# Retention with a rational feed-forward layer: blocks of one chunk from four batches, and one list schedule for all engines

## The chip, the cores and the metric

The kernel runs on one core of one Trainium2 chip. The metric is the time of one execution on the device in microseconds (us), the median of several runs. Engines are named as in the profile: PE (matrix products; PEld are its weight loads), DVE (vector), ACT (activation), POOL (GpSimd) and SP, which here only issues DMA transfers. Each engine works through its own queue of instructions in order and waits on semaphores for what others produce.

## The reference

Inputs are q, k and v of shape (4 batches, 8 heads, 768 positions, 64), two weight matrices (512 x 2048 and 2048 x 512), four numbers a and two numbers b. All is float32.

```python
for t in range(S):                                  # retention
    state = gamma * state + outer(k[:, :, t], v[:, :, t])
    y[:, :, t] = scale * (q[:, :, t] @ state)
x = y.transpose(0, 2, 1, 3).reshape(B * S, H * D)   # 3072 tokens x 512
h = x @ w_in
P = a[0] + a[1] * h + a[2] * h**2 + a[3] * h**3
Q = 1.0 + abs(b[0]) * abs(h) + abs(b[1]) * h**2
out = (P / (Q + 1e-06)) @ w_out
```

gamma differs by head, scale is 1/8.

## The kernel before, in words

**Retention in chunks.** The 768 positions of a batch are cut into C = 6 chunks of 128. For a chunk, `scores` (products at L254) multiplies k and q, `mask` (L261) multiplies by a causal mask into `aT`, `values_early` and `values_late` (L297, L308) multiply with v, and `recall` (L287) adds what the state of earlier chunks contributes, if there is one. `outer` (L274) makes the chunk's own k-v products and `update` (L317, L319) puts them into the state, which `scale_state` (L224, on POOL) decays. v is scaled by the decay in `scale_v` (L218, on POOL). The result `px` is scaled (L329) and split into a high part `xh` (L330, ACT) and a low part `xl` (L334, DVE), so that float32 accuracy comes out of products of two shorter parts.

**Blocks and slots.** Four consecutive chunks of 128 tokens make a block n of 512 tokens; there are 6 blocks, and 24 chunks numbered batch by batch, so block 0 is the first four chunks of batch 0, and block 1 the last two of batch 0 and the first two of batch 1. The hidden dimension has NF = 16 tiles f of 128. A slot is one pair (n, f), 96 in all: `gemm_in` (L392) makes twelve 128x128x512 products into `ph`; the rational function is worked out on ACT (L403, L409, L411, L420, L421), POOL (L410, sometimes L405) and DVE (L415, L416, L424, L425, L426); `split` (L431, L432) cuts the result into `gh` and `gl`; `gemm_out` (L447) makes twelve products into the four banks `po`. For the first two blocks the hidden tiles are done in two halves, block 0 f 0 to 7, block 1 f 0 to 7, then both again with f 8 to 15; the half sums go to DRAM and come back (`store`, `load_halves`).

**Weights.** 32 weight tiles (w_in and w_out by f) come as 64-bit words and are decoded on the chip: `decode_low` (L130, ACT) fills a buffer `t`, `decode_high` (L138, ACT) a PSUM bank `u`, `decode_join` (L146, L149, DVE) puts them together, `decode_split` (L159, ACT) and `decode_rest` (L166, POOL) make a high and a low part. `t` has three buffers.

**Order.** The order on every engine is written by hand. `opening()` does the first four chunks one after the other, with some products of zeros in between (`fill`, L350), and the first decodes. `run()` then goes through the slots k: the in-products of slot k, the out-products of slot k - 3 (LAG), the rational function of slot k, and in fixed places one decoded tile and a first or second half of a chunk of the next block (`parts`). SP issues loads in an order given by `FIRST`, `FETCH` and the calls of `load_rest`. Chunks 2 and 3 borrow buffers of the feed-forward part, which is not running yet. PSUM has eight banks: two for `ph`, two that scores, px and decodes take in turn, four for `po` (which the opening uses for other things).

Of the kernel before, what the change touches and what calls it, by code (L numbers as in the profile page):

```python
# [18 lines left out]


@with_exitstack
def tile_retention_rational_ffn(
# [9 lines left out]
    par: bass.AP,  # L32
    causal: bass.AP,
    xdec: bass.AP,
    vdec: bass.AP,
    sdec: bass.AP,
# [10 lines left out]
    NB = NSTEP // SPB  # L47

# [4 lines left out]
    ps_o = ctx.enter_context(tc.tile_pool(name="ps_o", bufs=1, space=PSUM))  # L53

    ps = ctx.enter_context(tc.tile_pool(name="ps", bufs=1, space=PSUM))

    o_tiles = {}
    count = {"ph": 0, "bank": 0, "u": 0}
    opened = []

    def bank(name, dtype=F32):
        tag = "ph" if name == "ph" else "bank"
        count[tag] += 1
        return ps.tile([P, TB], dtype, name=name, tag=f"{tag}{count[tag] % 2}")

    def early_bank(name, tag, dtype=F32):
        pool = ps_o if tag.startswith("po") else ps
        return pool.tile([P, TB], dtype, name=name, tag=tag)

    def u_bank():  # L70

        if not opened:
            return early_bank("u", "ph0", U32)
        if len(opened) < 2:
            count["u"] += 1
            return early_bank("u", f"po{count['u'] % 2}", U32)
        return bank("u", U32)

    def px_banks(i):
        if len(opened) < 2:  # L80
            return [early_bank("px", f"po{r + 2 * (i % 2 or i >= SPB)}") for r in range(2)]
        return [bank("px") for _ in range(2)]

# [3 lines left out]
    small = const.tile([P, H + NP + 10], F32, name="small")  # L87
    vdec_sb = small[:, :H]
# [5 lines left out]
    state = const.tile([P, NP, D], F32, name="state")  # L94
    zeros = ff.tile([P, DM], F32, name="zeros", tag="o", bufs=BUFS["o"]).bitcast(BF16)[:, :TB]
    wp = ctx.enter_context(tc.tile_pool(name="wp", bufs=1))
    w1, w2 = {}, {}
# [3 lines left out]
    lead, HF = 4, NF // 2  # L101
    tiles = []
    for h in range(0, NF, HF):
        tiles += [(0, h + f) for f in range(lead)]
        for f in range(h, h + HF):
            tiles += [(1, f)] + [(0, f + lead)] * (f + lead < h + HF)
    raws = []

    def fetch(count=1):
        for m, f in tiles[len(raws) : len(raws) + count]:  # L110
            raw = wp.tile([P, DM, 2], U32, name="raw", tag=f"w{m}_{f}")
            nc.sync.dma_start(
                out=raw.rearrange("p m w -> p (m w)"), in_=(w_in, w_out)[m][f]
            )
            raws.append(raw)

    us, ts = {}, {}

    def decode_read(i):
        decode_low(i)  # L120
        decode_high(i)

    def decode_low(i):
        if i >= len(tiles):
            return


        ts[i] = ff.tile([P, DM], U32, name="t", bufs=3)
        byte = raws[i].rearrange("p m w -> p (m w)").bitcast(U8)[:, 3::8]
        nc.scalar.activation(ts[i], byte, AF.Identity, bias=lcon[:, 0:1], scale=1.0 / 32)  # L130

    def decode_high(i):
        if i >= len(tiles):
            return


        us[i] = u_bank()
        nc.scalar.activation(  # L138
            us[i].bitcast(F32), raws[i][:, :, 1].bitcast(F32), AF.Abs, scale=2.0 ** -112
        )  # L140

    def decode_join(i):
        if i >= len(tiles):
            return
        u = us.pop(i)
        nc.vector.scalar_tensor_tensor(  # L146
            u, u, 3, ts[i], ALU.logical_shift_left, ALU.bitwise_or
        )
        nc.vector.scalar_tensor_tensor(  # L149
            ts[i], raws[i][:, :, 1], 0x80000000, u, ALU.bitwise_and, ALU.bitwise_or  # L150
        )

    def decode_split(i):
        if i >= len(tiles):
            return
        m, f = tiles[i]

        w = (w1, w2)[m][f] = wp.tile([P, 2, DM], F32R, name="w", tag=f"w{m}_{f}")
        nc.scalar.copy(w[:, 0], ts[i].bitcast(F32))  # L159

    def decode_rest(i):
        if i >= len(tiles):
            return
        m, f = tiles[i]
        w = (w1, w2)[m][f]
        nc.gpsimd.tensor_sub(w[:, 1], ts.pop(i).bitcast(F32), w[:, 0].bitcast(F32))  # L166


    steps = {}
    x_tiles = {}  # L170

    def x_block(n):
        if n not in x_tiles:
            x_tiles[n] = (
                xp.tile([P, NP, TB], F32R, name="xh"),
                xp.tile([P, NP, TB], F32R, name="xl"),
            )
        return x_tiles[n]

    borrowed = {2: ("gh", "gh", "q", "gl", "s"), 3: ("gh", "gl", "q", "gl", "s")}

    def landing(i, which, name, shape):
        if i in borrowed:
            tag = borrowed[i][which]
            full = ff.tile([P, TB], F32, name=name, tag=tag, bufs=BUFS.get(tag, 2))
            return full.rearrange("p (a b) -> p a b", b=shape[2])[:, : shape[1]]
        return at.tile(shape, F32, name=name)

    def load_part(i, n, src, which, shape):
        if i < NSTEP:
            st = steps.setdefault(i, {})
# [16 lines left out]

    def scale_v(i):
# [466 lines left out]
```

## Time and profile before

| what | value |
|---|---|
| median of 3 runs | 639.0 us (637.94 to 640.6) |
| profiled execution | 639.73 us, of it 638.0 us from the first to the last instruction (the span) |
| PE busy | 611.7 us (96% of the span), 4506 products |
| DVE, ACT, POOL busy | 452.9, 441.4 and 334.2 us |
| mean granted PE clock | 0.988 |
| moved by DMA | 55.11 MB, 86 GB/s over the span |

The profile is one execution. Its views are: a page with busy times and the costliest groups of instructions; groups by line; the timeline; busy times in chosen stretches of the span, with the PE clock that was granted in them; waits (who waited for whom); and a chain of work followed back from the last instruction. Times are us from the start of the span unless marked ns. A line number is one of the kernel as printed above. PE products overlap each other, and the ends of products are modelled, so the time of a set of products is read best from start to start.

### The profile page before, as it was taken

The page shows a single profiled execution, that of the slowest core. Times are in us where ns is not written, and L with a number is a line of the kernel's source. Part 1 is how long each engine was busy: PE and PEld are TensorE (multiplying, and loading weights), DVE is VectorE, ACT ScalarE, POOL GpSimd, SP SyncE. Part 2 cuts the span into 40 slices and gives each one's busy share as a digit, 9 for nine tenths or more (in the row PEclk, how much of TensorE's full clock was granted, in tenths as well). Part 3 has the DMA queues.
Part 4 walks back from the last instruction along what each step waited for, and adds up shares of the span by engine and source line. Part 5 has one row for each costly group of instructions (what it writes and reads, how often), then busy time and mean ns, then how long its engine had stood idle before and what let it go on. Part 6 is the DMA issues. An engine that isn't in the chain of part 4 may idle for free.

```text
span 638.0 us, 11577 instructions
## 1 busy us (share of the span) xinstructions
PE 611.7 (96%) x4506; PEld 494.4 (77%) x4510; DVE 452.9 (71%) x731; ACT 441.4 (69%) x721; POOL 334.2 (52%) x288
## 2 busy tenths in 40 slices
PE   6766999999999999999999999999999999999997
PEld 4655778888877878788888888888878888888885
DVE  3778688888888666785666777667766766666664
ACT  2488789888886665567666675766766666777773
POOL 1566568887875543454453454535354443444442
PEclk9887999999999999999999999999999999999999
DMA  8995563101015232320120311111311000100001
GB/s 306 393 370 174 192 241 141 44 1 66 1 45 180 87 96 85 124 76 17 59 59 17 116 44 61 48 27 54 112 40 43 2 0 1 42 25 2 0 2 66
DMA packets 27270, 55.11 MB, mean 86 GB/s; under 512 B 3408, under 2 KB 6096, under 8 KB 27216
## 3 DMA queue, kind: packets, MB, share of 16 engines
q1 hardware_dynamic: 27216, 54.38, 25.1%
q8 instruction: 35, 0.57, 0.4%
q14 instruction: 19, 0.16, 0.1%
HBM read 45.98 MB, written 8.39 MB: 85 GB/s over the span
## 4 chain that ended last, share of the span: by engine, by line
PE 67%; ACT 13%; DVE 11%; issue 5%; DMA 2%; POOL 1%; SPq 1%; POOLq 0%; DVEq 0%; ACTq 0%
PE po L447 30%; PE ph L392 30%; ACT t L130 3%; ACT s L420 2%; ACT ph L421 2%; DVE q L424 2%; PE pa L254 2%; DVE p L426 2%; DVE ph L425 2%; PE px L308 2%; DMA v<-in_v 2%; PE px L287 2%; PE px L274 1%; ACT u L138 1%; ACT s L409 1%
## 5 line engine op out<-in xcount | busy, mean ns | idle before, releaser
L410 POOL TENSOR_TENSOR q<-q,s 128x512 f32<-128x512 f32 x96 | 124.4, 1296 | 224.1 <-ACT s L409 215.4
L392 PE MATMUL ph<-xh,w 128*128 128x512 f32 (+2 forms) x776 | 210.4, 393 | 10.1 <-DVE p L426 5.7
L447 PE MATMUL po<-w,gh 128*128 128x512 f32 x768 | 201.4, 394 | 0.0
L392 PEld LDWEIGHTS ph<-xh,w 128*128 128x128 f32 x776 | 143.8, 188 | 42.5 <-DVE t L149 3.0
L447 PEld LDWEIGHTS po<-w,gh 128*128 128x128 f32 x768 | 143.4, 189 | 30.7 <-POOL w L166 0.2
L403 ACT ACTIVATE q<-ph 128x512 f32<-128x512 f32 x96 | 57.2, 596 | 111.3 <-PE ph L392 111.2
L415 DVE TENSOR_TENSOR p<-ph,p 128x512 f32<-128x512 f32 x96 | 66.2, 689 | 94.1 <-ACT p L411 94.1
L432 POOL TENSOR_TENSOR gl<-p,gh 128x512 fp32r<-128x512 f32 x96 | 124.4, 1295 | 9.7 <-ACT gh L431 3.8
L447 PE MATMUL po<-w,gl 128*128 128x512 f32 x384 | 111.1, 391 | 0.2 <-POOL gl L432 0.2
L424 DVE SCALAR_TENSOR_TENSOR q<-q,small,ph 128x512 f32<-128x512 f32 x96 | 71.4, 744 | 47.3 <-ACT ph L421 47.2
L392 PE MATMUL ph<-xl,w 128*128 128x512 f32 (+2 forms) x388 | 104.1, 390 | 0.0
L420 ACT ACTIVATE s<-q,small 128x512 f32<-128x512 f32 x96 | 69.4, 723 | 22.7 <-POOL q L410 22.7
L392 PEld LDWEIGHTS ph<-xl,w 128*128 128x128 f32 x388 | 73.2, 189 | 15.4
L447 PEld LDWEIGHTS po<-w,gl 128*128 128x128 f32 x384 | 72.5, 189 | 15.8 <-POOL gl L432 0.6
L416 DVE SCALAR_TENSOR_TENSOR p<-p,small,ph 128x512 f32<-128x512 f32 x96 | 71.8, 748 | 3.4
L411 ACT ACTIVATE p<-ph,small 128x512 f32<-128x512 f32 x96 | 73.2, 762 | 0.0
L425 DVE SCALAR_TENSOR_TENSOR ph<-p,small,ph 128x512 f32<-128x512 f32 x96 | 72.0, 750 | 0.0
L431 ACT CAST gh<-p 128x512 fp32r<-128x512 f32 x96 | 58.6, 610 | 16.7 <-DVE p L426 16.7
L426 DVE SCALAR_TENSOR_TENSOR p<-q,ph 128x512 f32<-128x512 f32 x96 | 65.9, 687 | 3.3
L409 ACT ACTIVATE s<-q,small 128x512 f32<-128x512 f32 x80 | 65.3, 816 | 2.7
L421 ACT ACTIVATE ph<-s 128x512 f32<-128x512 f32 x96 | 57.8, 602 | 9.9 <-DVE p L416 0.8
L218 POOL TENSOR_TENSOR v<-v,small 128x512 f32<-128x512 f32 x24 | 25.0, 1044 | 41.8 <-DMA v<-in_v 40.1
(41 smaller groups left out, 439.8 us busy)
## 6 DMA issues: line engine op xcount, KB each, us to landing
raw<-in_w_in SPq DMA_DIRECT2D x16, 512.0 KB, 5.7
raw<-in_w_out SPq DMA_DIRECT2D x16, 512.0 KB, 7.3
kT<-in_kT SPq DMA_DIRECT2D x24, 256.0 KB, 2.8
qT<-in_qT SPq DMA_DIRECT2D x24, 256.0 KB, 3.2
v<-in_v SPq DMA_DIRECT2D x24, 256.0 KB, 3.6
out<-o SPq DMA_DIRECT2D x24, 256.0 KB, 2.1
k<-in_k SPq DMA_DIRECT2D x20, 256.0 KB, 3.9
q2T<-in_q2T SPq DMA_DIRECT2D x20, 128.0 KB, 3.2
```

The lines of the kernel that those rows point to most:

```text
L392: nc.tensor.matmul(ph[:, t0:t1], w1[f][:, part, kt * P : (kt + 1) * P], x[:, kt, t0:t1], start=(i == 0), stop=(i == 3 * NP - 1),)
L409: nc.scalar.activation(s, q, AF.Identity, bias=babs[:, 0:1], scale=babs[:, 1:2])
L410: nc.gpsimd.tensor_mul(q, q, s)
L411: nc.scalar.activation(p, ph, AF.Identity, bias=par_sb[:, 2:3], scale=par_sb[:, 3:4])
L416: nc.vector.scalar_tensor_tensor(p, p, par_sb[:, 1:2], ph, ALU.add, ALU.mult)
L420: nc.scalar.activation(s, q, AF.Abs_reciprocal_sqrt, bias=qcon[:, 0:1])
L421: nc.scalar.activation(ph, s, AF.Square)
L424: nc.vector.scalar_tensor_tensor(q, q, qcon[:, 0:1], ph, ALU.add, ALU.mult)
L425: nc.vector.scalar_tensor_tensor(ph, p, par_sb[:, 0:1], ph, ALU.add, ALU.mult)
L426: nc.vector.scalar_tensor_tensor(p, q, 2.0, ph, ALU.subtract, ALU.mult, reverse0=True)
L432: nc.gpsimd.tensor_sub(gl, p, gh.bitcast(F32))
L447: nc.tensor.matmul(o_tiles[n][tt], g_[:, tt * P : (tt + 1) * P], w2[f][:, part], start=(first and m == 0), stop=(last and m == 2),)
```

## The change

1. **Block = the same chunk of four batches.** Chunk number i is now chunk c = i // 4 of batch i % 4. Block 0 holds the four first chunks, which have no state to recall and none of which depends on another; every batch has a state of its own (`state` is four times as large). Block 5 holds the four last chunks. Stores go to the rows of their batch.
2. **First chunks.** The mask for c = 0 (`mask0`, prepared on the host, 128 x 2 x 384) contains the decay and the scale, so `px` needs no scaling there and ACT and DVE split it at once. The outer products of the first chunks are not made with them, but in two steps of two batches each (`first_states`), with a DVE product that contains the decay of the state.
3. **Small inputs** (v's decay, the state's decay, a and b) come in one load.
4. **One list schedule.** Each piece of work is put down as a step with the engines that can do it, a cost in ns, what it comes after, the buffers it takes and uses, and a rank. `Plan.order` then simulates the engines on the host with these costs: it repeatedly takes, of the steps that can begin, the one that begins first, with a look-ahead of 100 to 300 ns on DVE, ACT and POOL within which the lower rank wins, and emits it on its engine. SP's loads are steps too, with a modelled rate and at most eight under way. The ranks are the slot numbers plus an offset for the kind of step, and for chunks and weight tiles a table of numbers; another table ranks the loads. `s` (the former L409 or L405) may go to ACT or POOL in the first 40 slots. In the opening, products of zeros fill modelled gaps of PE over 0.6 us.
5. **Buffers:** `t` has two instead of three; `q2T` one; the others as before.

The heart of the diff (the functions that issue instructions keep their bodies, apart from the points above):

```diff
+class Plan:
...
+    def order(self, emit):
...
+            by_engine = {}
+            for x in open_:
+                t = self.ready(x)
+                if t is None:
+                    continue
+                for e in x.engines:
+                    start = max(t, self.free.get(e, 0))
+                    if e == "SP" and len(self.landings) >= LANES:
+                        start = max(start, self.landings[-LANES])
+                    by_engine.setdefault(e, []).append((start, x))
+            best = None
+            for e, found in by_engine.items():
+                limit = min(f[0] for f in found) + LOOK.get(e, 0)
+                start, x = min((f for f in found if f[0] <= limit), key=lambda f: (f[1].rank, f[0]))
+                if best is None or start < best[0]:
+                    best = start, e, x
...
+            self.commit(x, e, start)
+            emit(x, e, gap)
...
-    def mask(i):
-        st = steps[i]
-        for s in range(2):
-            st["aT", s] = at.tile([P, 2, 3 * D], F32, name="aT")
-            nc.vector.tensor_mul(
-                st["aT", s], st["pa"][s],
-                causal_sb.rearrange("p x t -> p (x t)").unsqueeze(1).broadcast_to([P, 2, 3 * D]),
-            )
...
+            def mask(_, s=s):
+                st.setdefault("aT", {})[s] = at.tile([P, 2, 3 * D], F32, name="aT", bufs=BUFS["aT"])
+                by = causal_sb.rearrange("p x t -> p (x t)").unsqueeze(1).broadcast_to([P, 2, 3 * D])
+                if c == 0:
+                    by = masks[s].rearrange("p (j t) -> p j t", t=3 * D)
+                nc.vector.tensor_mul(st["aT"][s], st["pa"][s], by)
...
+    def first_states(b, rank, gate):
...
+        def run(_):
+            cell["pk"] = psum(pk, 0, "pk").rearrange("p (b h d) -> p b h d", b=2, d=D)
+            for x, st in enumerate((st0, st1)):
+                outer(st, cell["pk"][:, x], x == 0)
...
+        def update(_):
+            for x in range(2):
+                nc.vector.tensor_mul(
+                    state[:, b + x], cell["pk"][:, x],
+                    sdec_sb.unsqueeze(2).broadcast_to([P, NP, D]),
+                )
...
+        L = step(("ACT",), (651, 761), low, [got], rank, [t], kind="low")
+        U = step(("ACT",), (548, 623), high, [got, L], rank, [u], kind="high")
+        J = step(("DVE",), (1300, 1385), join, [L, U], rank, uses=[t, u], kind="join")
+        S = step(("ACT",), (509, 607), split, [J], rank, uses=[t], kind="split")
+        R = step(("POOL",), (1249, 1295), rest, [S], rank, uses=[t], kind="rest")
...
+        engines = ("ACT", "POOL") if k < SHARED else ("ACT",)
...
+        P1 = step(("POOL",), (1250, 1297), p1, [A2], k, uses=[q, s], kind="P1")
+        D1 = step(("DVE",), (1440, 1440), d1, [A3], k, uses=[p, ph], kind="D1")
+        A4 = step(("ACT",), (1265, 1327), a4, [P1, D1], k, uses=[q, s, ph], kind="A4")
+        D2 = step(("DVE",), (2030, 2100), d2, [A4, D1], k, uses=[p, q, ph], kind="D2")
...
+        O = step(
+            ("PE",), 2720, run_out,
+            [A6, (P2, slack), s1, (r1, slack), G, *gemms_out[-1:]], k,
+            [po] if first else [], [gh, gl] + ([] if first else [po]), kind="O",
+        )
...
-            dst = out[n * TB + tt * P : n * TB + (tt + 1) * P, :]
+                dst = out[(tt * C + n) * P : (tt * C + n + 1) * P, :]
...
-BUFS = {"gh": 3, "gl": 3, "o": 4}
-FETCH = 13
-FIRST = (1, 1, 1, 1, 3, 1)
-LAG = 3
-FILL = (10, 2)
+HOLD = 3000
+BUFS = {
+    "gh": 3, "gl": 3, "o": 4, "t": 2, "p": 2, "q": 2, "s": 2,
+    "kT": 2, "qT": 2, "q2T": 1, "k": 2, "v": 2, "aT": 2,
 }
...
+LOOK = {"ACT": 150, "DVE": 100, "POOL": 300}
+EARLY = 4
+SHARED = 40
+OFFSETS = {
+    "U": 0.333, "high": -2.618, "split": -2.404, "O": 7.966, "V": 0.44, "S": -3.954,
+    "M": -5.637, "R": -2.378, "XS": -0.298, "XH": 3.064, "XL": -4.337, "low": 0.086,
+    "join": 2.654, "rest": 2.845, "A1": -0.014, "A2": 0.571, "A3": -4.333, "P1": -4.315,
+    "D1": -0.384, "A4": -0.182, "D2": 0.694, "A6": -1.883, "P2": -1.29,
+}
```

Each chunk's steps are put down in `attention`, each weight tile's in `decode`, each pair (n, f) in `slot`; loads go through `load`. The first outer products have rank 1.108, so they compete with slot 1; the k of the first chunks is loaded behind their other inputs (`LATER`).

More of the change, by code (lines that the diff above doesn't have):

```diff
@@ L18, with __init__ @@
 TB = 512
+LANES = 8
+WAKE = 60
+ARRAY = 163
+ISSUE, LATENCY, LANDED, RATE = 470, 1850, 900, 380
+LEAVE, ENTER = 92, 111
+class Buffer:
+    def __init__(self, pool, options=None):
+        self.pool, self.options, self.banks = pool, options, None
+        self.users, self.end = 0, 0
+class Step:
+    def __init__(self, engines, cost, run, after, rank, takes, uses, tiled):
+        self.engines, self.cost, self.run, self.rank = engines, cost, run, rank
+        self.takes, self.uses, self.tiled = takes, [*takes, *uses], tiled
+        self.after = [(a, 0) if isinstance(a, Step) else a for a in after if a]
+        self.start = self.end = self.known = None
+        self.waits = 0
@@ L153, in decode_split @@
[L153 to L178, printed above, removed]
@@ L182, in tile_retention_rational_ffn @@
[L182 to L193, printed above, removed]
-            st[n] = landing(i, which, n, shape)
-            nc.sync.dma_start(out=st[n], in_=src[i // C, i % C])
@@ L222, in scale_state, with psum @@
[L222 to L226 removed]
+    plan = Plan({**BUFS, "x": 2}, [f"b{i}" for i in range(8)])
+    step = plan.step
+    nc.vector.memset(zeros, 0.0)
+    nc.vector.memset(qcon, 1.0 + 1e-6)
+    nc.vector.memset(lcon, -15.5 / 32)
+    nc.scalar.activation(babs[:, 0:1], qcon, AF.Abs_reciprocal_sqrt)
+    def psum(buffer, i, name, dtype=F32):
+        return ps.tile([P, TB], dtype, name=name, tag=buffer.banks[i])
@@ new lines, in tile_retention_rational_ffn, with begun, free_banks, pairs @@
+    gemms_in, gemms_out, po_now, former = [], [], {}, {}
+    def begun(n):
+        return len(gemms_in) >= n and gemms_in[n - 1].start is not None
+    def free_banks():
+        names = ["b2", "b3"]
+        if not begun(EARLY):
+            names += ["b4", "b5", "b6", "b7"]
+        if not begun(1):
+            names += ["b0"]
+        return names
+    def pairs():
+        names = free_banks()
+        return [names[i : i + 2] for i in range(0, len(names) - 1, 2)]
+    def load(dst, src, nbytes, rank, takes=(), uses=(), after=()):
+        cell = {}
+        def run(_):
+            cell["tile"] = dst()
+            nc.sync.dma_start(out=cell["tile"], in_=src())
+        x = step(("SP",), (ISSUE, max(nbytes / RATE, 190)), run, after, rank, takes, uses)
+        return x, cell
@@ L437, in gemm_out, with gemm_in @@
+    o_tiles = {}
+    def gemm_in(cell, n, f, t0, t1):
+        xh, xl = x_tiles[n]
+        i = 0
+        for part, x in ((0, xh), (0, xl), (1, xh)):
+            for kt in range(NP):
+                nc.tensor.matmul(
+                    cell["ph"][:, t0:t1], w[0, f][:, part, kt * P : (kt + 1) * P], x[:, kt, t0:t1],
+                    start=(i == 0), stop=(i == 3 * NP - 1),
+                )
+                i += 1
+    def gemm_out(cell, n, f, first, last, po):
         if first:
-            o_tiles[n] = [ps_o.tile([P, DM], F32, name="po", tag=f"po{i}") for i in range(SPB)]
@@ L476, in tile_retention_rational_ffn, with load_sums @@
+    def load_sums(n, gate):
+        for tt in range(SPB):
+            o = Buffer("o")
+            x, cell = load(
+                lambda: ff.tile([P, DM], F32, name="o", bufs=BUFS["o"]), lambda tt=tt: halves[n, tt],
+                4 * P * DM, 0.0, [o], after=[(gate, None), stores[n, 0, tt]],
+            )
+            sums[n, tt] = o, cell, x
     order = [(n, f) for h in range(2) for n in range(2) for f in range(h * HF, (h + 1) * HF)]
     order += [(n, f) for n in range(2, NB) for f in range(NF)]
-    nslot = len(order)
@@ L479, in tile_retention_rational_ffn @@
-    groups = {
-        (n, f): (f == 0 or (n < 2 and f == HF), f == NF - 1 or (n < 2 and f == HF - 1))
-        for n, f in order
-    }
-    parts = {}
+    starts = {}
     for n in range(1, NB):
```

833 lines of the change are left out of this document (475 added, 358 removed), and 19 rows, old and new, of tables (LOADS, RANKS).

## The prediction

> **What bounds the kernel now.** A slot is one hidden tile f of one block n: 12 products into `ph` (L392), the rational function on ACT, DVE and POOL, and 12 products into `po` (L447). There are 96. I read the busy time by stretches first (per engine: busy us, count in brackets; then granted TensorE clock, DMA share, GB/s).
>
> ```profile
> core 0 of [0], span 638.0 us
> 0.00:26.00 26.00, 18.97 (x382) 12.62 (x386) 12.57 (x31) 8.63 (x17) 8.60 (x14) 0.93 0.94 339
> 26.00:93.00 67.00, 54.21 (x528) 43.12 (x522) 52.69 (x92) 52.26 (x91) 40.44 (x35) 0.92 0.71 253
> 93.00:623.00 530.00, 527.54 (x3559) 430.25 (x3559) 381.88 (x602) 375.00 (x607) 281.33 (x238) 1.00 0.17 53
> ```
>
> The columns are PE, weight loads, DVE, ACT, POOL. From 93 us on PE is busy 527.5 of 530 us: no order of the other engines can give back more than those 2.5 us. Before that it isn't the bound. The chain of waits in the steady part gives PE's prices (start, us, what):
>
> ```profile
> 295.26 0.81 PE pa L254 x24
> 296.07 2.96 PE ph L392 x12
> 299.03 2.72 PE po L447 x12
> 301.75 2.72 PE ph L392 x12
> 304.47 0.60 PE px L287 x16
> 305.07 0.23 PE px L297 x16
> 305.30 0.61 PE px L308 x16
> 305.92 0.47 PE px L274 x16
> ```
>
> A set of 12 products is 2.72 us. A chunk's scores cost 0.81 plus 0.24 on the products behind (2.96 against 2.72): 1.05. Its second burst is 0.60 + 0.23 + 0.61 + 0.47 = 1.91, with the same 0.24 it is 2.15; together 3.2. So how much of 26 to 93 us was needed? The same stretch, for line 392 and then for line 447 alone:
>
> ```profile
> 26.00:93.00 67.00, 26.51 (x108) 20.12 (x108) 0.92 0.71 253
> 26.00:93.00 67.00, 16.22 (x60) 12.23 (x60) 0.92 0.71 253
> ```
>
> Slot 0 is cut in two (24 products), so 108 is eight slots, and 60 is five sets of `po`: 13 x 2.72 = 35.4, and four chunks at 3.2 = 12.8, in all 48.2 of 67 us. Some 19 us are lost here, and 26 us go by before. The whole question is when slot 8 begins: now at 93 us.
>
> **The opening.** The timeline of PE:
>
> ```profile
> 26.11 0.96 PE L392 MATMUL ph<-xh,w 128*128 128x384 f32 x4
> ...
> 29.61 0.82 PE L392 MATMUL ph<-xh,w 128*128 128x128 f32 x4 [1.14 <-ACT xh L330]
> ...
> 31.33 0.90 PE L254 MATMUL pa<-qT,kT 64*64 64x128 f32 x32
> 35.10 1.23 PE L392 MATMUL ph<-xh,w 128*128 128x512 f32 x3 [2.87 <-DVE t L149]
> ```
>
> Slot 0 runs from 26.11 to 31.33. The change asks less before it: the four first chunks belong to four batches, so there is no recall, no state that waits for its forerunner, no `k` and no `q2T` to load; `k` goes behind. Four chunks of three loads of 128 x 512 f32 (0.262 MB), two masks of 128 x 384 f32 (0.197 MB) and one weight tile of 128 x 1024 words (0.524 MB) are 4.06 MB; without the fourth chunk 3.28 MB.
>
> ```profile
> 0.00:18.00 18.00, 11.77 (x220) 7.20 (x222) 7.39 (x19) 5.41 (x10) 3.66 (x8) 1.00 0.89 317
> ```
>
> By 18 us 317 GB/s x 18 = 5.7 MB have been moved, by 26 us 339 x 26 = 8.8 (the first view): 3.1 in 8 us, 0.39 MB per us. So 3.28 MB are there at 18 - 2.42/0.39 = 11.8 us, 4.06 MB at 13.8. Next the prices of DVE, which carries most, of the decode on ACT, and of the scaling of v on POOL (line, engine, operation, tiles; busy us, mean ns; idle before it):
>
> ```profile
> L425 DVE SCALAR_TENSOR_TENSOR ph<-p,small,ph 128x512 f32<-128x512 f32 x96 | 72.0, 750 | 0.0
> L416 DVE SCALAR_TENSOR_TENSOR p<-p,small,ph 128x512 f32<-128x512 f32 x96 | 71.8, 748 | 3.4
> L424 DVE SCALAR_TENSOR_TENSOR q<-q,small,ph 128x512 f32<-128x512 f32 x96 | 71.4, 744 | 47.3 <-ACT ph L421 47.2
> L415 DVE TENSOR_TENSOR p<-ph,p 128x512 f32<-128x512 f32 x96 | 66.2, 689 | 94.1 <-ACT p L411 94.1
> L426 DVE SCALAR_TENSOR_TENSOR p<-q,ph 128x512 f32<-128x512 f32 x96 | 65.9, 687 | 3.3
> L261 DVE TENSOR_TENSOR aT<-pa,causal_sb 128x384 f32<-128x384 f32 x48 | 24.6, 552 | 7.1 <-PE pa L254 7.0
> L146 DVE SCALAR_TENSOR_TENSOR u<-u,t 128x512 uint32<-128x512 uint32 x32 | 22.2, 693 | 7.1 <-ACT u L138 7.1
> L149 DVE SCALAR_TENSOR_TENSOR t<-raw,u 128x512 uint32<-128x512 uint32 x32 | 22.0, 688 | 1.3
> L334 DVE TENSOR_TENSOR xl<-px,xh 128x256 fp32r<-128x256 f32 x48 | 18.2, 420 | 7.1 <-ACT xh L330 6.9
> L329 DVE TENSOR_TENSOR px<-px,xdec_sb 128x256 f32<-128x256 f32 x48 | 18.1, 423 | 0.0
> ```
>
> ```profile
> L130 ACT ACTIVATE t<-raw,small 128x512 uint32<-128x512 uint8 x33 | 25.1, 761 | 6.2 <-DMA raw<-in_w_in 6.2
> L138 ACT ACTIVATE u<-raw 128x512 f32<-128x512 f32 x33 | 20.6, 623 | 0.0
> L159 ACT CAST w<-t 128x512 fp32r<-128x512 f32 x32 | 19.4, 611 | 7.6 <-DVE t L149 7.6
> L330 ACT CAST xh<-px 128x256 fp32r<-128x256 f32 x48 | 16.2, 371 | 10.1 <-DVE px L329 9.5
> ```
>
> ```profile
> L218 POOL TENSOR_TENSOR v<-v,small 128x512 f32<-128x512 f32 x24 | 25.0, 1044 | 41.8 <-DMA v<-in_v 40.1 <-PE ph L392 1.6
> ```
>
> The first weight tile is decoded in 0.76 + 0.62 + 0.69 + 0.69 + 0.61 = 3.4 us: slot 0 can start at 11.8 + 3.4 = 15.2. Its last quarter needs the fourth chunk: landed at 13.8, then v scaled (1.04), the values (0.23 + 0.61 in the chain), high parts (2 x 0.37) and low parts (2 x 0.42): 17.3; that piece itself took 1.7 (29.61 to 31.33). Slot 0 ends near 19 instead of 31.3. That is 12 us, if PE were all that counted.
>
> **To slot 8.** PE's floor is 15.2 + 35.4 + 12.8 and the two pairs of first outer products, moved here out of the opening (2 x (2 x 0.47 + 0.24) = 2.4): 65.8 us. DVE's floor is later. Before slot 8 it owes: the five operations of seven slots and two of the eighth, 7 x 3.62 + 1.44 = 26.8; joins of 8 w_in tiles and 5.5 w_out tiles (five sets of `po`, half the next) at 1.38, 18.6; masks of eight chunks, 8 x 2 x 0.55 = 8.8; low parts, 8 x 0.84 = 6.7; scaling of x for the four later chunks alone (the first four have it in the mask, 3.4 us saved), 3.4; four state updates and four products for the first states, taken at the 0.42 of the same size, 3.4. Together 67.7. By the time slot 0 ends (19 us) data have let it do the first masks, low parts and one join: 4.4 + 3.4 + 1.4 = 9.2. The other 58.5 follow: with no gap slot 8 begins at 19 + 58.5 = 77.5. How full can an in-order DVE be? From 26 to 93 us it was 52.7/67 = 0.79; that share would give 93, the time of now. The point of the change is that the order of all engines is planned from the durations and the tiles' landing times, and not in fixed groups per slot; ACT, which was as full (52.3), may also hand the `s` of a slot to POOL (40.4). I take 0.96, near the upper end because the queue of ready work (decodes, which wait for nothing but DMA) is long in this stage: 19 + 58.5/0.96 = 80 us, 13 us earlier than now. Ends: 65.8 (PE) and 93.
>
> DMA: before slot 8 come 14 weight tiles (7.3 MB), four chunks (1.18 MB each with q2T and k), 1.05 MB of k, 0.35 of constants and the 4.06: 17.5 MB, at 0.39 MB/us about 48 us. SP's queue is ordered by the same plan, so a load whose buffer is not free is put behind others; the k loads that are moved behind delay weight 1 by 2.7 us, while PE has the first outer products to do. Hidden, but worth 2.7 if not.
>
> One more term: with slots of (80 - 19)/8 = 7.6 us in this stage and a chain from `ph` to `gl` of 8.9 us (in the last slot the products of `ph` end where the next set starts, at 622.60, and `gl` at 631.49),
>
> ```profile
> 622.60 1.98 PE L447 MATMUL po<-w,gh 128*128 128x512 f32 x8
> ```
>
> ```profile
> 630.20 1.29 POOL L432 TENSOR_TENSOR gl<-p,gh 128x512 fp32r<-128x512 f32 x1 [3.31 <-issue]
> ```
>
> slot 8 finds six sets of `po` done and not five: PE has 2.7 us less left. After slot 8 all is PE: every chunk is now recalled (two were first chunks of their batch: + 2 x 0.60), four instead of three have no outer product (- 0.47): + 0.7. Of the 2.5 us of idle PE after 93 I count 1.0 as won by earlier loads (bounds 0 and 2.5). The last products, copies and stores keep their work, and a store still writes 128 whole rows: 0. POOL loses the four scalings of the first states, which the DVE products now contain: 0, it is the least busy engine (281 of 530 us in the first view).
>
> Sum on the profiled execution (639.73, of which 638.0 are span; the three runs went from 637.94 to 640.6): - 13.1 - 2.7 + 0.7 - 1.0 = - 16.1, that is 621.9 of span and 623.6 of time. That execution is 0.7 above the median of 639.0, so I forecast 623.
>
> **The clock.** From 26 to 93 us the granted clock is 0.92, a loss of 0.08 x 67 = 5.4 us, and 1.00 after that. From 19 to 80 us PE has 61 us for the remaining 48, so the same loss would fit in and the forecast doesn't change; only an outcome at PE's floor would pay it (65.8 becomes 71.2). [...]
>
> **Rivals.**
> Better: the plan keeps DVE gapless, and starts of operations overlap a little, so slot 8 begins at 66 to 75. That is 639.0 - 18.1 - 3.0 = 618 down to 639.0 - 27.3 - 3.0 = 609. For it: decodes are independent work. Against it: ACT is nearly as full and shares every chain with DVE, and the clock above. 0.15.
> Half: an engine takes its instructions in the order of its queue, so an operand that comes later than planned holds all that stands behind it. With a share of 0.84, half of the way back, slot 8 is at 19 + 58.5/0.84 = 88.6, without the sixth `po`: - 4.5 + 0.7 - 1.0, 634; the case goes from 627 to 635.8. For it: DVE now waits 94.1 and 47.3 us over the run for ACT's `p` and `ph`, so a late ACT reaches it at once. Against it: these waits lie mostly where PE is the bound anyway. 0.17.
> Hidden: the earlier slot 0 gives nothing, since DVE keeps its 0.79 and slot 8 stays at 93: 639.0 + 0.7 - 1.0 = 638.7, or 639.7 without the 1.0. For it: ACT as full as DVE. 0.05.
> Slower: decoding is starved of its buffer. `t` goes from three buffers to two, and a tile holds one from its first reading to the end of its rest:
>
> ```profile
> 38.98 0.75 ACT L130 ACTIVATE t<-raw,small 128x512 uint32<-128x512 uint8 x1
> ```
>
> ```profile
> 45.88 1.30 POOL L166 TENSOR_TENSOR w<-t,w 128x512 fp32r<-128x512 f32 x1
> ```
>
> 8.2 us. With two, 13.5 tiles take 13.5 x 4.1 = 55 us from 11.8 on, which just fits before 80. At a hold of 12 us it is 11.8 + 81 = 93 and the gain is gone; at 13.2 slot 8 begins at 101 and the time is 639.0 + 7.9 + 0.7 - 1.0 = 647. For it: the longer the look-ahead, the longer a half-decoded tile waits. Against it: the plan knows the buffers. 0.08.
>
> **Numbers.** 0.55 for the forecast (DVE's share 0.90 to 1: slot 8 at 77.5 to 84, so 639.0 - 15.6 - 3.0 = 620 to 639.0 - 9.1 - 3.0 = 627, and 618 with all 2.5 us of idle PE won), 0.15, 0.17, 0.05, 0.08 for the rivals. A measurement here tells 0.5% (3.2 us) from no change. Faster by more: 0.55 + 0.15 + 0.17 = 0.87; same 0.05; slower 0.08. The range 610 to 635 leaves out the last two and the lowest part of the better case.
>
> **What would show it.** Right: the first `ph` product near 15 us, the first state products behind it, slot 8 (the ninth set of `ph`) near 80 with DVE 0.95 busy between, PE without gaps after. Wrong: slot 8 near 93 with DVE waiting on ACT's decode (buffers), PE waiting on DMA before 50 us (loads), or idle PE after slot 8, which now has 2.5 us of it.

## The result and the profile after

| | before | after |
|---|---|---|
| median of 4 runs each | 639.51 us (637.94 to 640.6) | 624.57 us (624.17 to 624.92) |
| profiled span | 638.0 us | 622.4 us |
| mean granted PE clock | 0.988 | 0.994 |
| slot 8 begins (ninth set of `ph`) | 93.07 us | 83.69 us |
| from there to the end of the span | 544.9 us | 538.7 us |

The ratio is 0.977 (95% interval 0.9745 to 0.9791): 15 us faster. Of the 15.6 us of span, 9.4 were won before slot 8 and 6.2 behind it. Line numbers from here on are those of the changed kernel; `ph` products stand in L586, `po` in L601, the recall in L316, the values in L325 and L333, the joins in L556 and L559, the rest of a weight tile in L568, the last step of the rational function (`p`) in L677.

The busy time by stretches, as for the kernel before (us, then PE, weight loads, DVE, ACT, POOL, then granted clock, DMA share, GB/s):

```profile
core 0 of [0], span 622.4 us
...
0.00:26.00 26.00, 20.62 (x368) 15.44 (x371) 13.08 (x30) 11.08 (x23) 7.88 (x12) 1.00 0.96 341
26.00:93.00 67.00, 59.49 (x575) 47.23 (x574) 59.09 (x100) 56.24 (x97) 53.51 (x49) 0.95 0.78 298
93.00:623.00 530.00, 525.11 (x3568) 428.62 (x3566) 375.85 (x595) 353.15 (x580) 286.72 (x246) 1.00 0.15 50
```

In the second row every engine has risen: PE from 54.2 to 59.5 us, DVE from 52.7 to 59.1, POOL from 40.4 to 53.5. The same stage cut finer shows where PE is still not full:

```profile
19.00:27.00 8.00, 8.00 (x84) 6.85 (x84) 6.12 (x12) 6.65 (x12) 3.28 (x3) 1.00 1.04 391
27.00:36.00 9.00, 5.50 (x122) 4.78 (x126) 7.31 (x12) 7.77 (x15) 8.65 (x9) 0.74 1.03 400
36.00:47.00 11.00, 7.42 (x47) 5.52 (x43) 10.09 (x18) 8.96 (x17) 5.66 (x6) 0.90 1.04 398
47.00:60.00 13.00, 13.00 (x141) 10.70 (x134) 11.49 (x21) 10.28 (x18) 9.44 (x10) 1.00 1.03 402
60.00:70.00 10.00, 10.00 (x128) 8.02 (x127) 8.91 (x17) 7.89 (x14) 8.58 (x9) 1.00 1.01 392
70.00:84.00 14.00, 13.57 (x112) 10.20 (x112) 13.04 (x23) 12.72 (x23) 11.35 (x11) 1.00 0.51 174
```

From 47 us on PE is busy 36.6 of 37 us: there it is the bound, with DVE next to it. Nearly all that PE loses behind slot 0 lies between 27 and 47 us, in idle PE and in a granted clock of 0.74 and 0.90. The waits of PE from slot 0 to slot 8:

```profile
PE px L316 <- DMA q2T<-in_q2T: 2.8, 1, 2.8
PE ph L586 <- DVE p L677: 2.4, 1, 2.4
PE px L316 <- DVE t L559: 1.9, 2, 1.2
PE po L601 <- POOL w L568: 0.4, 1, 0.4
```

That is 7.5 us of waits; the half clock takes up to 3.4 more (0.26 x 9 + 0.10 x 11). The DMA engines are full up to 70 us (share 1.01 to 1.04), and yet PE waits for a landing only once here, for q2T. Whether faster loads would bring slot 8 forward was not tried.

### The profile page after: what moved, and what is told of

It reads as the page before. It is cut to its first block, busy times and chain, and to the rows that moved or that the text cites. A ratio compares the mean times of both kernels' runs of the same rounds, so it can differ in the third digit from the quotient of the medians.

```text
span 622.4 us, 11626 instructions
## 1 busy us (share of the span) xinstructions
PE 605.2 (97%) x4507; PEld 491.3 (79%) x4509; DVE 448.0 (72%) x723; ACT 420.5 (68%) x698; POOL 348.1 (56%) x305
## 4 chain that ended last, share of the span: by engine, by line
PE 89%; DVE 1%; POOL 1%; DMA 0%; ACT 0%; issue 0%; SPq 0%; DVEq 0%
PE po L601 41%; PE ph L586 40%; PE pa L300 2%; PE px L333 2%; PE px L316 2%; PE px L306 1%; PE px L325 1%; DMA v<-in_v 0%; DVE q L675 0%; DVE p L677 0%; DVE t L559 0%; DVE ph L676 0%; POOL w L568 0%; POOL q L659 0%; POOL s L644 0%
## 5 line engine op out<-in xcount | busy, mean ns | idle before, releaser
L586 PE MATMUL ph<-xh,w 128*128 128x512 f32 (+2 forms) x776 | 210.0, 393 | 2.8 <-DVE p L677 2.8
L601 PE MATMUL po<-w,gh 128*128 128x512 f32 x768 | 200.4, 392 | 0.4 <-POOL w L568 0.4
L586 PEld LDWEIGHTS ph<-xh,w 128*128 128x128 f32 x776 | 143.3, 188 | 34.7 <-ACT p L654 2.8
L601 PEld LDWEIGHTS po<-w,gh 128*128 128x128 f32 x768 | 142.5, 188 | 31.7 <-POOL w L568 1.4
L601 PE MATMUL po<-w,gl 128*128 128x512 f32 x384 | 110.4, 389 | 0.0
L668 ACT ACTIVATE s<-q,small 128x512 f32<-128x512 f32 x96 | 69.4, 723 | 52.9 <-POOL q L659 52.7
L586 PE MATMUL ph<-xl,w 128*128 128x512 f32 (+2 forms) x388 | 103.2, 388 | 0.0
L586 PEld LDWEIGHTS ph<-xl,w 128*128 128x128 f32 x388 | 72.7, 188 | 15.2
L601 PEld LDWEIGHTS po<-w,gl 128*128 128x128 f32 x384 | 72.1, 188 | 15.0
L654 ACT ACTIVATE p<-ph,small 128x512 f32<-128x512 f32 x96 | 74.5, 776 | 4.2 <-POOL gl L687 4.2
L677 DVE SCALAR_TENSOR_TENSOR p<-q,ph 128x512 f32<-128x512 f32 x96 | 65.9, 686 | 3.3
L568 POOL TENSOR_TENSOR w<-t,w 128x512 fp32r<-128x512 f32 x32 | 41.3, 1292 | 12.9 <-ACT w L565 12.7
L644 POOL TENSOR_SCALAR s<-q,small 128x512 f32<-128x512 f32 x37 | 28.5, 771 | 35.2 <-ACT q L639 35.0
```

The lines of the kernel that those rows point to most:

```text
L586: nc.tensor.matmul(cell["ph"][:, t0:t1], w[0, f][:, part, kt * P : (kt + 1) * P], x[:, kt, t0:t1], start=(i == 0), stop=(i == 3 * NP - 1),)
L601: nc.tensor.matmul(o_tiles[n][tt], g_[:, tt * P : (tt + 1) * P], w[1, f][:, part], start=(first and m == 0), stop=(last and m == 2),)
L654: nc.scalar.activation(cell["p"], cell["ph"], AF.Identity, bias=par_sb[:, 2:3], scale=par_sb[:, 3:4])
L668: nc.scalar.activation(cell["s"], cell["q"], AF.Abs_reciprocal_sqrt, bias=qcon[:, 0:1])
L677: nc.vector.scalar_tensor_tensor(p_, q_, 2.0, ph_, ALU.subtract, ALU.mult, reverse0=True)
```

## The experiments

They ask three things: which part of the change brings the gain (regrouping, list, tables), whether DVE is what sets slot 8, and what the half clock costs. Beside each time stands its ratio to the kernel before, run on the same chip. Different kernels ran on different chips, so a difference between two of them is given by the medians and, where it matters, also by the ratios. "Slot 0 / slot 8 / rest" is when the first `ph` product and the ninth set begin and how long the span goes on after that; for the changed kernel it is 19.3 / 83.7 / 538.7, for the kernel before 26.1 / 93.1 / 544.9.

### The grouping alone, in the old order

The kernel before, with the new numbering, one state per batch and the stores to match; for room `o` has three buffers and q2T one, loaded late.

```diff
+    chunk_of = [i // B for i in range(NSTEP)]
...
-    state = const.tile([P, NP, D], F32, name="state")
+    state = const.tile([P, B, NP, D], F32, name="state")
...
-            nc.sync.dma_start(out=st[n], in_=src[i // C, i % C])
+            nc.sync.dma_start(out=st[n], in_=src[i % B, chunk_of[i]])
...
-BUFS = {"gh": 3, "gl": 3, "o": 4}
+BUFS = {"gh": 3, "gl": 3, "o": 3}
```

> The kernel before with its order written by hand, but a block is the same chunk of four batches (a state per batch, no recall in the first block). No mask with decay, no list schedule. To make room for the larger state, q2T has one buffer and its load is issued a chunk later, and o has three buffers. Theory (the list order carries the gain, the grouping alone little): the opening loses recalls and state waits, slot 0 begins 3 to 5 us earlier than 26, but the slots up to slot 8 stay as loosely filled as before, so 634 to 639 us. Rival (the grouping carries it): slot 8 comes 8 us earlier or more, 631 us or less.

655.55 us, ratio 1.026 (1.0226 to 1.0289); 24.1 / 92.6 / 561.8. The loss of 17 us lies behind slot 8, where PE waits only 2.7 us in the kernel before. The timeline of PE at the change of a block:

```profile
207.79 1.07 PE L395 MATMUL ph<-xh,w 128*128 128x512 f32 x4
213.35 0.95 PE L289 MATMUL px<-qT,state 64*64 64x128 f32 x5 [4.49 <-DVE aT L263]
```

PE waits 4.49 us for a mask, and some 6.8 us at half clock go with it (the granted clock is 0.91 from 200 to 240 us). Each of the losses (near 112, 159, 206 and 271 us) lies where half sums come back, which go through `o`, and `o` had one buffer less: the suspicion is that this spoils the run, and not the grouping. So once more, with `o` at four buffers and the room taken from `k`, which is loaded late too:

```diff
-        return at.tile(shape, F32, name=name)
+        return at.tile(shape, F32, name=name, bufs=1 if name in ("q2T", "k") else 2)
...
+                load_again(chunk + 1)
+                load_k(chunk + 1)
```

> The hand-ordered kernel with blocks of one chunk from four batches again, now with four buffers o as in the kernel before: room for the larger state comes from one buffer each for q2T and k, whose loads go out behind the burst that frees them. Theory (the 16 us which the first form lost after slot 8 came from its three o buffers at the half sums; the grouping alone does nearly nothing): slot 8 at 92 to 93 as in the first form, 636 to 641 us. Rival (the grouping itself disturbs the hand order): 648 us or more.

636.2 us, ratio 0.9956 (0.9933 to 0.9979); 23.8 / 90.5 / 543.9. The loss behind slot 8 is gone, which bears the suspicion out. In the old order, with its mask and its scaling, the grouping is worth some 3 us, of the 15.

### The list alone, on the old blocks and on the new

The list schedule with the offsets of the kinds of steps, but with the two tables of ranks empty; first with blocks of four consecutive chunks and one state, the mask and the scaling as before:

```diff
-        n, b = divmod(i, B)
...
+        n, s = divmod(i, SPB)
...
-        st, (n, b) = {}, divmod(i, B)
-        c, own = n, state[:, b]
+        st, (n, at_), (b, c) = {}, divmod(i, SPB), divmod(i, C)
+        own = state[:, 0]
...
-    "kT": 2, "qT": 2, "q2T": 1, "k": 2, "v": 2, "aT": 2,
+    "kT": 2, "qT": 2, "q2T": 2, "k": 2, "v": 2, "aT": 2,
...
+LOADS = {}
+RANKS = {}
```

> The list schedule with the offsets kept and the other two tables empty, on blocks of four consecutive chunks as in the kernel before: one state, recalls and state updates in the opening, the first outer products with their chunk, x scaled by DVE everywhere, the causal mask everywhere, two q2T buffers. Its partner with the grouping is offsets_only (643.5 us). Theory (the grouping frees the opening, which by hand was worth 2.8 us): 645 to 652 us, slot 0 begins at 25 us or later. Rival (the grouping is worth nothing to the list): 641 to 645 us; other rival: under 640 us, the grouping hurts.

645.46 us, ratio 1.009 (1.0066 to 1.0119); 26.3 / 93.9 / 550.3. Then the changed kernel itself, with the offsets kept:

```diff
-LOADS = {
-    0: -7.6272, 1: -16.9199, 2: -7.6029, 3: -7.0202, 4: 0.0115, 5: 0.018, 6: 0.1, 7: 0.1478,
...
-RANKS = {
-    0: -21.328, 1: -7.141, 2: -0.123, 3: -13.1, 4: -0.418, 5: -0.474, 6: -12.839, 7: 6.65,
...
+LOADS = {}
+RANKS = {}
```

> The changed kernel with the offsets by kind of step kept, the ranks of chunks and weights and the load ranks empty. Theory (the offset of the out-products, 7.97 slots, lets the in-products go first and so keeps the rational function's chain ahead of PE; that is what the empty tables lacked after slot 8, and the two tables by chunk and tile are worth only the order of the opening): PE without gaps after slot 8, 626 to 640 us. Rival (the rank tables are what counts): 660 us or more.

643.51 us, ratio 1.006 (1.003 to 1.0081); 23.1 / 92.6 / 545.7. That lies between what I had put for the theory and for its rival. The nine runs go from 639.61 to 645.71 us, and the profiled one (640.08) is a quick one, so its three stage times are short by some 3 us in sum. The list with the offsets alone is thus 0.6 to 0.9% slower than the old order by hand, on the old blocks and on the new; between the two the grouping, with its mask and its first outer products, makes 2 us, with intervals that overlap.

### No table at all, and one number of it

The same with the offsets gone too, so that a step ranks by its slot alone:

```diff
-OFFSETS = {
-    "U": 0.333, "high": -2.618, "split": -2.404, "O": 7.966, "V": 0.44, "S": -3.954,
...
-}
+OFFSETS = {}
```

> The changed kernel with its three tables (ranks, offsets by kind, load ranks) empty, so that chunks, weights and slots are ranked by the slot that needs them. Theory (the list and the grouping carry the gain, the table a few us of it): slot 8 begins 2 to 6 us later than 83.7, 626 to 632 us. Rival (the table is what makes it): 634 us or more; other rival (the table is worth nothing): within 2 us of 624.6.

682.37 us, ratio 1.069 (1.0644 to 1.074); 23.3 / 89.9 / 587.5. My theory was off by 50 us. The kernel reaches slot 8 earlier than the kernel before and then loses 43 us. (The same with the old blocks has no measured time.) The waits of PE from 93 us on:

```profile
PE ph L586 <- DVE p L677: 33.0, 21, 4.2
```

and its timeline around one of them:

```profile
400.65 1.98 PE L601 MATMUL po<-w,gh 128*128 128x512 f32 x8
402.46 1.07 PE L601 MATMUL po<-w,gl 128*128 128x512 f32 x4
403.37 1.07 PE L586 MATMUL ph<-xh,w 128*128 128x512 f32 x4
404.28 1.07 PE L586 MATMUL ph<-xl,w 128*128 128x512 f32 x4
405.18 1.07 PE L586 MATMUL ph<-xh,w 128*128 128x512 f32 x4
407.81 1.19 PE L586 MATMUL ph<-xh,w 128*128 128x512 f32 x4 [1.56 <-DVE p L677]
```

Read it from below. The `ph` set at 407.81 needs a bank of `ph`, of which there are two, and the function of the slot two before holds it until `p`. PE has no `po` set left to fill the time: it did that at 400.65, ahead of the `ph` set at 403.37, because a `po` set belongs to an older slot and so ranked first whenever both could begin. In-products that come later make the function's chain later, and no work is in reserve when it is waited for. So I put back one number of the 23, the one that lets `po` rank 8 slots later:

```diff
-OFFSETS = {}
+OFFSETS = {"O": 7.966}
```

> All tables empty but for one number, the offset 7.966 of the out-products. Theory (this one number removes the 33 us that PE waited for ph after slot 8 with empty tables, since slot k + 2's in-products wait for the function of slot k and must not stand behind out-products): 640 to 652 us, PE waits for ph under 5 us after slot 8. Rival (other kinds, ACT's order above all, are behind it): 670 us or more.

646.31 us, ratio 1.011 (1.008 to 1.0138); 23.6 / 96.1 / 548.4. The waits for `p` behind 93 us fall from 33.0 to 4.9 us, and 36 us come back (37 by the ratios). The other 22 offsets make 2.8 more, with intervals that touch. In the order by hand LAG, the three slots between the in-products and the out-products, has this part.

### Which table: loads or steps

The changed kernel with the table of loads and the offsets kept, and the ranks gone. I held that the order of the loads carries the gain; the rival was the order in which ACT and DVE take up tiles and chunks.

```diff
-RANKS = {
-    0: -21.328, 1: -7.141, 2: -0.123, 3: -13.1, 4: -0.418, 5: -0.474, 6: -12.839, 7: 6.65,
...
+RANKS = {}
```

> The changed kernel with offsets and load ranks kept and the ranks of chunks and weight tiles empty. Against offsets_only (643.5 us) and the changed kernel (624.6 us) it divides those 19 us. Theory (DMA is saturated for the first 60 us, so the order of loads carries most of the 19 us): 626 to 632 us. Rival (the ranks of decodes and chunks on the engines carry it): 637 us or more.

643.4 us, ratio 1.005 (1.0034 to 1.0069); 19.5 / 96.7 / 544.2. My theory fell. Slot 0 begins as early as with both tables, so that is what the loads' table does, and by slot 8 it is all lost again. One stretch of this kernel, to be held against the same one above:

```profile
60.00:70.00 10.00, 8.04 (x84) 6.03 (x83) 3.39 (x6) 4.63 (x8) 4.73 (x4) 0.83 1.02 404
```

and PE within it:

```profile
63.17 3.62 PE L601 MATMUL po<-w,gh 128*128 128x512 f32 x8 [1.96 <-ACT w L565]
```

PE is held up by a w_out tile whose split has just ended, and DVE is busy 3.4 of 10 us where it was 8.9: the in-products of the next slot stand behind this `po` set, so no function runs and nothing else is at hand. The longest wait of this kernel before slot 8 ends in the same way:

```profile
PE ph L586 <- ACT w L565: 5.2, 1, 5.2
```

That the wrong tile was decoded next is how I read these two waits; no run changes the rank of one tile alone. With the same loads the ranks of chunks and tiles take 643.4 to 624.6: 18.8 us (18 by the ratios), more than the whole gain. The reverse, ranks of steps without those of the loads, wasn't tried; nor was a table made for the old blocks, so what the tables would give without the grouping is open.

### Is DVE the bound before slot 8?

Three kernels with the changed kernel's order, untouched: one with less work on DVE, one with more, one with more on ACT. In the first the first operation of the join writes `t` and the second is left out in the first 14 tiles (14 x 0.69 = 9.7 us):

```diff
+            joined.append(tag)
+            if len(joined) <= 14:
+                nc.vector.scalar_tensor_tensor(
+                    t_, u_, 3, t_, ALU.logical_shift_left, ALU.bitwise_or
+                )
+                return
```

> The changed kernel with its order untouched, but the first 14 decoded weight tiles leave out the second joining operation on DVE (these weights lose their sign): 14 x 0.69 = 9.7 us less of DVE before slot 8, nothing else. Theory (DVE's work sets the start of slot 8): slot 8 begins 6 to 10 us earlier, at 74 to 78, and 615 to 619 us. Rival (landing times or ACT or the fixed order set it): slot 8 moves by less than 3 us, 622 to 625 us.

623.42 us, ratio 0.977 (0.9744 to 0.9798); 19.7 / 83.1 / 538.7. DVE's busy time from 26 to 93 us fell from 59.1 to 53.0; slot 8 came 0.6 us earlier, and by the ratios (0.977 both times) nothing was won. The theory that DVE sets slot 8 falls. PE's waits from slot 0 to slot 8 in this run tell why:

```profile
PE px L316 <- DMA q2T<-in_q2T: 3.4, 1, 3.4
PE ph L592 <- ACT s L654: 2.3, 1, 2.3
```

The wait for q2T doesn't come from DVE, and the other one now ends on ACT. The opposite, with the second operation of the join done twice:

```diff
+            for _ in range(2 if len(joined) <= 14 else 1):
+                nc.vector.scalar_tensor_tensor(
```

> The changed kernel with its order untouched and the second joining operation of the first 14 weight tiles made twice: 14 x 0.69 = 9.7 us more of DVE before slot 8. Taking them away moved nothing, so DVE isn't the bound; this asks how near it is. Theory (DVE was busy 57 of 64.7 us from 19 us to slot 8, so 7.7 us of slack take most of it): slot 8 1 to 5 us later, 625 to 630 us. Rival (each operation added on the chain of decode, join and product is paid in full): 632 us or more.

631.87 us, ratio 0.988 (0.9849 to 0.9904); 19.1 / 89.7 / 540.0. Of 9.7 us added to DVE 7.3 reach the time (7.0 by the ratios), a value between what I had put for the theory and for its rival. The half clock lasts 3.4 us longer than in the changed kernel (granted clock 0.70, 0.81 and 0.97 from 27 to 36, 36 to 47 and 47 to 60 us, where that has 0.74, 0.90 and 1.00), so up to 1.7 us of them are the clock's. PE now waits for DVE:

```profile
PE ph L588 <- DVE p L679: 5.3, 4, 3.7
PE px L316 <- DVE t L561: 4.8, 4, 2.2
```

And ACT's split done twice in the same tiles (14 x 0.61 = 8.5 us):

```diff
+            for _ in range(2 if len(joined) <= 14 else 1):
+                nc.scalar.copy(w[m, f][:, 0], cell["t"].bitcast(F32))
```

> The changed kernel with its order untouched and the split on ACT of the first 14 weight tiles made twice: 14 x 0.61 = 8.5 us more of ACT before slot 8 (ACT is busy some 54 of 65 us there). The same amount on DVE cost 7.3 us of time, taking it away gained nothing. Theory (the tuned order leaves several engines equally near to the limit, not DVE alone): slot 8 4 to 8 us later, 628 to 633 us. Rival (DVE alone is near it): under 627 us.

627.53 us, ratio 0.980 (0.977 to 0.9829); 20.1 / 85.8 / 540.6: 2 to 3 us, at the edge between what I had put for the two sides; slot 8 comes 2.1 us later, where the theory had 4 to 8. Its one long wait is

```profile
43.23 2.05 PE L588 MATMUL ph<-xh,w 128*128 128x512 f32 x4 [6.01 <-ACT p L656]
```

In this order DVE thus stands just under the limit: what is added counts for three quarters, what is taken away counts for nothing. ACT has more room. The order was planned for the old durations; what one planned for the longer ones would lose was not tried.

### What the half clock costs

The changed kernel's timeline of PE, around the two waits:

```profile
31.96 0.70 PE L316 MATMUL px<-q2T,state 64*64 64x128 f32 x8 [2.77 <-DMA q2T<-in_q2T]
...
42.59 1.15 PE L586 MATMUL ph<-xh,w 128*128 128x512 f32 x4 [2.38 <-DVE p L677]
```

The granted clock is half (0.50) from 31.3 to 38.1 us. I put 28 products of zeros ahead of chunk 4's recall, into a half of its bank that is not used, so that PE is at work while it waits; 3.2 us, and nothing depends on them:

```diff
+            for _ in range(28 if i == B else 0):
+                nc.tensor.matmul(
+                    st["px"][0][:, TB // 2 :], zeros[:, :P], zeros[:, : TB // 2], start=True, stop=True,
+                    skip_group_check=True,
+                )
```

> The changed kernel with 28 products of zeros (128x256, into an unused part of the bank) ahead of chunk 4's recall, where PE waits for q2T up to 31.96 us and the clock falls to half from 31.3 to 38.1. Revised theory (PE's own queue is gapless from 47 us on, so what PE loses before that sets slot 8; the half clock takes some 3 us of it): granted clock 1.00 there, slot 8 1.5 to 3.5 us earlier than 83.7, 621 to 623 us. Rival (PE waits for others in this stage anyway): slot 8 and the time within 0.7 us of the changed kernel's.

621.96 us, ratio 0.973 (0.971 to 0.975); 19.1 / 82.2 / 538.0. The four runs (621.37 to 622.85) lie below all four of the changed kernel; 2.6 us by the medians, 2.4 by the ratios, whose intervals touch; slot 8 comes 1.5 us earlier. The same two stretches as above:

```profile
27.00:36.00 9.00, 8.07 (x162) 6.80 (x155) 8.52 (x15) 7.82 (x15) 8.66 (x8) 1.00 1.03 402
36.00:47.00 11.00, 7.84 (x80) 5.89 (x80) 10.56 (x19) 9.74 (x18) 7.29 (x8) 0.84 1.03 396
```

The clock is full in the first and now falls in the second, behind the next wait:

```profile
27.61 3.23 PE L435 MATMUL px<-o 128*128 128x256 bf16 x28
...
32.15 0.45 PE L316 MATMUL px<-q2T,state 64*64 64x128 f32 x8 [0.93 <-DMA q2T<-in_q2T]
...
40.85 1.17 PE L591 MATMUL ph<-xh,w 128*128 128x512 f32 x4 [3.16 <-DVE p L682]
```

The q2T lands no earlier (32.15, before that 31.96), so what was won is the clock's. The wait up to 40.85 was filled too, with 13 products of zeros ahead of slot 3's in-products, into a bank that is free then:

```diff
+                if k == 3:
...
+                    for _ in range(13):
+                        nc.tensor.matmul(fill, zeros[:, :P], zeros, start=True, stop=True)
```

> As no_half_clock, with 13 more products of zeros (128x512, into a free bank) ahead of slot 3's in-products, where PE waits 3.16 us for the function of slot 1 and the clock falls to half at 42.3 us. Theory (a wait of some 3 us is paid twice, as idle time and as half clock behind it): no half clock before the end, slot 8 at 80.5 to 81.7, 620.3 to 621.5 us. Rival (the second half-clock stretch costs nothing, PE waits for others there): 621.6 to 622.4 us.

622.34 us, ratio 0.973 (0.9699 to 0.9754); 18.9 / 81.5 / 539.2.

```profile
36.00:47.00 11.00, 9.35 (x96) 6.25 (x96) 10.62 (x18) 10.66 (x19) 7.55 (x8) 1.00 1.04 398
```

The clock is full through the whole stage, and the time is that of one filled gap: the second one, some 3.4 us at half clock (0.84 over 11 us), cost nothing that can be measured. The two kernels with filled gaps are the fastest of all that ran, faster than both kernels of this case; between the two there is no difference.

## Why the prediction was right, and where it was not

The forecast was 623.0 us and 624.57 came, but two of its terms are wrong and nearly cancel: slot 8 came 3.7 us later than put (83.69 for 80), and the stage behind it was 3.2 us shorter than put. That the time came within 1.6 us of the forecast is thus in part luck.

**Where the gain lies: right in the main.** Of 15.6 us, 9.4 come before slot 8 and 2.7 are the sixth `po` set, which is done before it; 3.5 are of the stage behind. What the argument said is that no order can win much there; that an order can lose much there (587.5 without offsets, 550 on the old blocks) was not in it.

**Slot 0 at 15.2: too early by 4.1 us.** Two steps failed. The decode was priced without the rest on POOL, 1.27 us, which the third group of products needs, and the data of the first chunks were taken to land in the order in which they are wanted. POOL, DVE and PE of the changed kernel:

```profile
16.12 1.04 POOL L394 TENSOR_TENSOR v<-v,small 128x512 f32<-128x512 f32 x1 [3.65 <-DMA v<-in_v]
17.12 1.27 POOL L568 TENSOR_TENSOR w<-t,w 128x512 fp32r<-128x512 f32 x1
```

```profile
18.13 0.74 DVE L494 TENSOR_TENSOR xl<-px,xh 128x256 fp32r<-128x256 f32 x2
```

```profile
15.51 0.90 PE L300 MATMUL pa<-qT,kT 64*64 64x128 f32 x32 [1.84 <-DMA qT<-in_qT]
16.20 0.44 PE L325 MATMUL px<-aT,v 64*64 64x64 f32 x16
...
19.26 0.96 PE L586 MATMUL ph<-xh,w 128*128 128x384 f32 x4
```

The fourth chunk's scores stand on PE ahead of the third chunk's values, and wait for a qT until 15.51; the third chunk's masks had been done at 14.3. Its low parts, which the second group of products of slot 0 needs, so end at 18.87. On POOL the rest of the first weight tile stands behind the scaling of a v that lands at 16.12, and ends at 18.39, ahead of those low parts: the third chunk came last, not the decode. SP had issued a weight tile (0.52 MB) at 6.80, that qT at 7.72 and that v at 8.54, and then, at 9.39, the four loads of `k` (1.05 MB), which I had counted behind the first weight tiles:

```profile
6.80 0.33 SPq L264 DMA_DIRECT2D raw<-in_w_in  x1
...
7.72 0.53 SPq L264 DMA_DIRECT2D qT<-in_qT  x1
8.54 0.33 SPq L264 DMA_DIRECT2D v<-in_v  x1
9.39 2.31 SPq L264 DMA_DIRECT2D k<-in_k  x4
```

That qT and that v took 7.8 and 7.5 us to land, while these kinds take 6.1 and 5.0 at the median of the first 20 us. The `k` loads behind them look like the cause, but the kernel with the offsets alone speaks against it: there four `k` loads follow at 8.84 on a qT and a v issued at 7.50 and 8.17, which both land after 5.4 us, and no weight tile stands ahead of them. In the changed kernel itself the v issued at 6.28, ahead of the weight tile, took 5.1 us and the kT issued at 7.17, behind it, 7.5. The weight tile ahead is thus the likelier cause; no run changes it alone.

**DVE's share sets slot 8: wrong.** This is the step that failed. "The other 58.5 follow" on DVE at a share of 0.96 gave 80; DVE was busy 57.0 of the 65 us from 19 to 84, 0.88, so the amount of its work was right and the share was not, and taking 9.7 us of it away moved slot 8 by 0.6 us. What sets slot 8 is PE itself from 47 us on, and before that a chain with single waits: for q2T (a load), for `p` and `t` (DVE), and the clock. That several engines are near their limit at once would explain the asymmetry of the two DVE runs, but it isn't shown: 8.5 us more on ACT cost only 2 to 3.

**The clock costs nothing: wrong by 2.4 to 2.6 us.** I wrote that the loss "would fit in", on the ground that DVE was the bound. That fell with its premise: with the first gap filled the time went down. In the changed kernel the clock is half from 31.28 to 38.10 us, beginning within the wait of 2.77 us (up to 31.96); with that wait filled it was full there (1.00 from 27 to 36 us). What that is worth the runs say: 2.4 to 2.6 us the first time, nothing the second. In the kernel before the clock is below 1 in the first 26 us as well (0.93): it is half from 18.56 to 21.97 us, and the waits of PE ahead of that are 1.44 us at most (up to 7.61), the last 1.26 (up to 18.30).

**Behind slot 8: the mechanism right, a size too small.** Put at -2.7 + 0.7 - 1.0 = -3.0, measured -6.2. Six sets of `po` are done before slot 8, as forecast. PE's waits behind 93 us were 2.7 us in the kernel before:

```profile
PE ph L392 <- DVE p L426: 1.6, 3, 1.0
PE px L287 <- DVE t L149: 0.4, 1, 0.4
PE ph L392 <- ACT xh L330: 0.3, 1, 0.3
PE px L287 <- DVE aT L261: 0.2, 1, 0.2
PE po L447 <- POOL gl L432: 0.2, 1, 0.2
```

Now there is one of 0.4:

```profile
PE ph L586 <- DVE p L677: 0.4, 1, 0.4
```

That is -2.3 where I had put -1.0. The other 1.9 us are not waits. Added up from start to start, the products of the 16 chunks behind slot 8 take 42.0 us where they took 42.5, and I had put 0.7 more: that is 1.2 of them. The other 0.7 lie in the out-products and were not followed up.

**Hiding places and rivals.** Of the rivals' mechanisms that of "Half" is seen (an operand later than planned holds all that stands behind it: the qT up to 15.51 above), at a smaller price. "Slower" by the two buffers of `t` did not come; three buffers were not tried. What would have made this change slower was something else, which the prediction did not name: the rank of the out-products, one number, at 36 us. And the prediction gave the credit to the planning as such ("planned from the durations and the tiles' landing times"): with its ranks empty the plan has the same durations, landing times and buffers, and is 0.6 to 6.9% slower than the kernel before.

**What the gain is made of.** In the order in which I took the parts away: list without any table +44 us against the kernel before, on the new blocks; the offset of the out-products -36, the other offsets -3, the loads' ranks 0, the ranks of chunks and tiles -19. The tables were kept as the change has them, so each of these holds beside the others; other values of the offsets might do better with empty ranks. The mask with the decay, the one load of the small inputs and the numbers of buffers were not tried alone.

## What to carry to other kernels

A list scheduler that takes "the oldest slot first" lets the consumer of a finished chain go ahead of the producer that starts the next one; give the producer the better rank and keep the consumer's work as a reserve (36 us here). An engine at 88% beside a bound of another kind is tested from both sides: less work on it won nothing, more cost three quarters of what was added. Before a wait of PE that can't be removed, products that nothing needs are worth a try, and the gain has to be measured for each one: here it was 2.4 to 2.6 us for a wait of 2.77 us and nothing for one of 3.16.

## What the runs showed of the hardware

In the kernel before the granted clock is half (0.50) from 18.56 to 21.97, from 35.63 to 39.03 and from 56.11 to 62.93 us, and 1.00 in the rest of the first 93 us. In the changed kernel it is half from 31.28 to 38.10 us, and 1.00 before that and from there to 83 us.

The length of a wait of PE alone doesn't decide whether half clock comes. In these two traces it began during a wait of 2.77 us (up to 31.96, changed kernel), behind one of 2.87 (up to 35.10, before) and during one of 1.98 (up to 56.90, before) that follows one of 2.00 (up to 54.52). It did not follow a wait of 2.38 us (up to 42.59, changed kernel) or one of 2.36 (up to 43.98, before). In the other runs:

| wait of PE | up to | run | what the trace has around it |
|---|---|---|---|
| 1.96 us | 63.17 us | the loads' ranks without the ranks of steps | clock 0.83 from 60 to 70 us |
| 2.35 us | 41.77 us | less on DVE | clock 0.84 from 36 to 47 us |
| 3.16 us | 40.85 us | first gap filled | clock 0.84 from 36 to 47 us |
| 4.49 us | 213.35 us | the grouping by hand, three buffers `o` | clock 0.91 from 200 to 240 us |
| 6.01 us | 43.23 us | more on ACT | four products behind it take 1.85 us from start to start, at 52.77 us 0.90 |

What sets the wait of 2.38 us apart from that of 1.96 no run shows.

With DMA at 328 GB/s, as in the first 20 us of the changed kernel, a load of 0.26 MB of q, k or v took 5.0 to 7.4 us to land, by the median of its kind, and up to 7.8.
